# Two x loads merged on ScalarE, and the first transposes and gate projection put in order of landing, in a SwiGLU kernel

## Chip, cores, metric

One core of one Trainium2 chip. The metric is device time in microseconds (us). Quoted are medians of several executions. The kernel before took 164.04 us (164.0 to 164.34, three runs).

## The reference

```python
B, S, D, F = 1, 2048, 640, 1536            # bfloat16
def reference(x, w_gate, w_up, w_down):
    g = jax.nn.silu(x @ w_gate)
    u = x @ w_up
    return (g * u) @ w_down
```

## The kernel before

Rows are worked on in four blocks of 512. Projections need x transposed. Blocks 1 to 3 get it by a transposing DMA. Block 0 is in a hurry: its four 128-row chunks are loaded plainly, transposed on TensorE into PSUM and copied to SBUF by VectorE and ScalarE. Until the data is there TensorE runs "fillers", matmuls on a tile of ones that nobody reads.

```python
    queues = (nc.sync, nc.scalar)
    halves = ((0, KD // 2 + 1), (KD // 2 + 1, KD))        # k 0-2 on SyncE, 3-4 on ScalarE
    for c in (0, 1):
        for i, eng in enumerate(queues):
            load_x(eng, c + 2 * i, c + 2 * i + 1)         # SyncE: chunks 0, 1; ScalarE: 2, 3
    for dst, src in ((wg_sb, wg_v), (wu_sb, wu_v)):       # first 128 columns of the weights
        for eng, (k0, k1) in zip(queues, halves):
            eng.dma_start(out=dst[:, k0:k1, wslice(0, 1)], in_=src[:, k0:k1, wslice(0, 1)])
    load_w(nc.sync, wg_sb, wg_v, *W_CHUNKS[1])            # "second gate piece", columns 128-383
    # ... [cut: table load, second up piece, all other weights, transposing loads]

    def transpose_chunk(c, parts):
        for copy, tag, k0, k1 in parts:                   # po_a, po_b: two PSUM buffers each
            pt = psum.tile([P, k1 - k0, P], bf16, tag=tag, name="pt")
            # ... [cut: k1 - k0 TensorE transposes of x_sb[:, c] into pt]
            copy(out=xT[:, k0:k1, c_sl], in_=pt[:])

            if sb == 0 and fc == 0:                       # first column block of row block 0
                warm(N_WARM)                              # 18 fillers
                transpose_chunk(0, [(dve, "po_a", 0, KD)])
                transpose_chunk(2, [(dve, "po_b", 0, KD)])
                warm(N_GAP)                               # 4
                for c in (1, 3):
                    transpose_chunk(c, [(act, "po_a", 0, 2), (dve, "po_b", 2, KD)])
                warm(2)
                proj_pair(pg, wg_sb, fc, sb, 0)           # gate, chunks 0 and 2
                proj_pair(pg, wg_sb, fc, sb, 1)           # gate, chunks 1 and 3
                proj(pu, wu_sb, fc, sb, 0, S_BLK)         # up, all
            else:                                         # "second block" is fc == 1
                proj(pg, wg_sb, fc, sb, 0, S_BLK)
                proj(pu, wu_sb, fc, sb, 0, S_BLK)
            # ... [cut: silu on ScalarE, product on VectorE; then the down projection]
```

## Time and profile before

| | kernel before |
|---|---|
| median time | 164.04 us |
| span in the trace | 162.8 us |
| TensorE busy | 159.0 us (98%) |
| first gate projection starts | 5.05 us |
| second block starts | 7.25 us |

A line of the chain of waits gives start, length and what held the end at that time. A line of the timeline gives start, length, engine, source line, operation and count, and in square brackets the idle time before it with what ended it. The spacing of TensorE's instructions is read from such a line as (length minus the 0.22 to 0.31 us that one of them takes) over (count minus 1), or directly from the starts in the trace. From the second block on the matmuls follow each other without a gap, so what can change is when the second block starts. The prediction shows the lines.

### The profile page before, as it was taken

How to read it: one execution, taken by the hardware profiler on the slowest of the kernel's cores; microseconds unless marked ns; L12 is line 12 of the kernel's file. 1: busy time of each engine (PE TensorE's matmuls, PEld its weight loads, DVE VectorE, ACT ScalarE, POOL GpSimd, SP SyncE). 2: the span in 40 equal slices, each digit the busy share in tenths (PEclk: the TensorE clock that was granted, in tenths of full speed). 3: DMA queues.
4: the chain of work that ended last, by engine and by line, in shares of the span. 5: the costliest groups of instructions: out<-in, count | busy, mean ns of one | idle time of the engine just before them, and what ended most of it. 6: DMA issues, size and time to landing. Idle time of an engine off the chain costs nothing.

```text
span 162.8 us, 1869 instructions
## 1 busy us (share of the span) xinstructions
PE 159.0 (98%) x766; PEld 75.3 (46%) x781; DVE 37.9 (23%) x58; ACT 42.4 (26%) x72; POOL 0.6 (0%) x6
## 2 busy tenths in 40 slices
PE   8999999999999999999999999999999999999994
PEld 7644444444444444444444444444444444445442
DVE  2322333310022333311002333331001333332000
ACT  3322222112222222221222222221213222222121
POOL 1000000000000000000000000000000000000000
PEclk9999999999999999999999999999999999999999
DMA  7999999804100000003110000000320000000302
GB/s 214 244 327 328 361 236 226 161 9 80 45 32 0 0 0 0 4 0 34 64 64 0 2 4 0 0 0 5 60 68 32 0 0 0 0 0 4 56 33 72
DMA packets 26888, 11.26 MB, mean 69 GB/s; under 512 B 17664, under 2 KB 26880, under 8 KB 26880
## 3 DMA queue, kind: packets, MB, share of 16 engines
q1 hardware_dynamic: 17968, 10.16, 22.8%
q10 hardware_dynamic: 8912, 0.98, 3.9%
q8 instruction: 6, 0.10, 0.3%
q14 instruction: 2, 0.02, 0.0%
HBM read 6.55 MB, written 2.62 MB: 56 GB/s over the span
## 4 chain that ended last, share of the span: by engine, by line
PE 96%; DMA 2%; issue 1%; SPq 0%; DVE 0%
PE pu L134 31%; PE pg L134 31%; PE po_a L213 25%; PE po_t L189 6%; DMA x_sb<-in_x_dram 2%; PE pg L149 1%; PE pt L125 0%; PE po_b L226 0%; SPq L74 0%; DVE ot_b L234 0%; PE pw L103 0%
## 5 line engine op out<-in xcount | busy, mean ns | idle before, releaser
L134 PE MATMUL pu<-xT,wu_sb 128*128 128x512 bf16 x230 | 58.9, 379 | 0.5
L134 PE MATMUL pg<-xT,wg_sb 128*128 128x512 bf16 x235 | 58.4, 379 | 0.0
L181 DVE TENSOR_TENSOR aT<-sg,pu 128x512 bf16<-128x512 f32 x48 | 33.1, 689 | 100.5 <-PE pu L134 100.5
L180 ACT ACTIVATE sg<-pg 128x512 f32<-128x512 f32 x48 | 28.7, 597 | 71.1 <-PE pg L134 70.1
L213 PE MATMUL po_a<-wd_sb,aT 128*128 128x512 bf16 x188 | 41.9, 379 | 0.2
L134 PEld LDWEIGHTS <-wu_sb 128*128 128x128 bf16 x240 | 23.5, 98 | 28.1 <-DMA wu_sb<-in_w_up_dram 0.2
L134 PEld LDWEIGHTS <-wg_sb 128*128 128x128 bf16 x235 | 22.9, 98 | 27.8 <-DMA wg_sb<-in_w_gate_dram 0.4
L213 PEld LDWEIGHTS <-aT 128*128 128x128 bf16 x192 | 18.8, 98 | 22.6
L221 ACT CAST ot<-po_a 128x512 bf16<-128x512 f32 x16 | 9.4, 585 | 32.4 <-PE po_a L213 19.3
L189 PE MATMUL po_t<-aT,wd_sb 128*128 128x512 bf16 (+1 forms) x47 | 10.3, 365 | 0.1
L189 PEld LDWEIGHTS <-wd_sb 128*128 128x128 bf16 x48 | 4.7, 98 | 5.1
L198 ACT CAST ot_t<-po_t 128x512 bf16<-128x512 f32 (+1 forms) x4 | 2.2, 558 | 11.6 <-PE po_t L189 11.6
L199 DVE STREAM_TRANSPOSE ot_q<-ot_t 128x512 bf16<-128x512 bf16 (+1 forms) x4 | 2.7, 678 | 9.0 <-ACT ot_t L198 9.0
L103 PE MATMUL pw<-ones 128*128 128x128 bf16 x24 | 2.8, 289 | 0.4 <-DVE ones L78 0.4
L234 DVE CAST ot_b<-po_b 128x128 bf16<-128x128 f32 x1 | 0.3, 291 | 9.9 <-PE po_b L226 9.9
L103 PEld LDWEIGHTS <-ones 128*128 128x128 bf16 x24 | 2.3, 136 | 0.4 <-DVE ones L78 0.4
L130 DVE COPY xT<-pt 128x640 bf16<-128x640 bf16 (+1 forms) x4 | 1.6, 424 | 3.5 <-PE pt L125 3.5
L125 PE MATMUL pt<-ident,x_sb 128*128 128x128 bf16 x20 | 1.9, 262 | 0.5 <-DMA x_sb<-in_x_dram 0.5
L125 PEld LDWEIGHTS <-x_sb 128*128 128x128 bf16 x20 | 1.5, 119 | 0.9 <-DMA x_sb<-in_x_dram 0.9
L89 ACT ACT_TABLE_LOAD x1 | 1.3, 1283 | 2.0 <-issue 2.0
L149 PE MATMUL pg<-xT,wg_sb 128*128 128x256 bf16 x10 | 1.3, 272 | 0.0
L149 PEld LDWEIGHTS <-wg_sb 128*128 128x128 bf16 x10 | 0.9, 98 | 0.1
(11 smaller groups left out, 3.5 us busy)
## 6 DMA issues: line engine op xcount, KB each, us to landing
out_dram<-ot SPq DMA_DIRECT2D x16, 128.0 KB, 1.7
wd_sb<-in_w_down_dram SPq DMA_DIRECT2D x1, 1920.0 KB, 12.0
wg_sb<-in_w_gate_dram SPq DMA_DIRECT2D x3, 480.0 KB, 7.7
wu_sb<-in_w_up_dram SPq DMA_DIRECT2D x3, 480.0 KB, 8.1
out_dram<-ot_q ACTq DMA_DIRECT2D x12, 32.0 KB, 1.9
x_sb<-in_x_dram SPq DMA_DIRECT2D x2, 160.0 KB, 3.1
x_sb<-in_x_dram ACTq DMA_DIRECT2D x2, 160.0 KB, 3.3
wg_sb<-in_w_gate_dram SPq DMA_DIRECT2D x1, 320.0 KB, 4.4
```

The lines of the kernel that those rows point to most:

```text
L103: nc.tensor.matmul(pw[:, 0:P], lhsT=ones[:], rhs=ones[:], start=True, stop=True)
L125: nc.tensor.transpose(out=pt[:, kd - k0, :], in_=x_sb[:, c, kd * P : (kd + 1) * P], identity=ident[:],)
L130: copy(out=xT[:, k0:k1, c_sl], in_=pt[:])
L134: nc.tensor.matmul(ps[:, c0:c1], lhsT=w_sb[:, kd, fc * P : (fc + 1) * P], rhs=xT[:, kd, sb * S_BLK + c0 : sb * S_BLK + c1], start=(kd == 0 ...
L149: nc.tensor.matmul(pair(ps[:]), lhsT=w_sb[:, kd, fc * P : (fc + 1) * P], rhs=pair(xT[:, kd, sb * S_BLK : (sb + 1) * S_BLK]), start=(kd == ...
L180: nc.scalar.activation(sg[:], pg[:], ACT.Silu)
L181: nc.vector.tensor_tensor(out=aT[:, fc, s_sl], in0=sg[:], in1=pu[:], op=ALU.mult)
L189: nc.tensor.matmul(po_t[:], lhsT=wd_sb[:, kf, DA:D], rhs=aT[:, kf, sb * S_BLK : sb * S_BLK + n_t], start=(kf == 0), stop=(kf == KF - 1),)
L198: nc.scalar.copy(ot_t[:], po_t[:])
L199: nc.vector.transpose(out=ot_q[:], in_=ot_t[:])
L213: nc.tensor.matmul(po_a[:], lhsT=aT[:, kf, s0 : s0 + P], rhs=wd_sb[:, kf, 0:DA], start=(kf == 0), stop=(kf == KF - 1),)
L221: nc.scalar.copy(ot[:], po_a[:])
```

## The change

The intent: one load for chunks 2 and 3, so that they land together and early, and TensorE's work in the order in which the chunks then land, 0, 2, 3, 1. The first half of the gate projection covers chunks 2 and 3, the other half 0 and 1.

```diff
-    N_WARM, N_GAP = 18, 4
+    N_WARM, N_GAP = 18, 5
-    for c in (0, 1):
-        for i, eng in enumerate(queues):
-            load_x(eng, c + 2 * i, c + 2 * i + 1)
+    load_x(nc.sync, 0, 1)
+    load_x(nc.scalar, 2, SUB)
+    load_x(nc.sync, 1, 2)
... [cut: proj_pair removed]
                 transpose_chunk(0, [(dve, "po_a", 0, KD)])
+                warm(N_GAP)
                 transpose_chunk(2, [(dve, "po_b", 0, KD)])
-                warm(N_GAP)
-                for c in (1, 3):
+                for c in (3, 1):
                     transpose_chunk(c, [(act, "po_a", 0, 2), (dve, "po_b", 2, KD)])
                 warm(2)
-                proj_pair(pg, wg_sb, fc, sb, 0)
-                proj_pair(pg, wg_sb, fc, sb, 1)
+                proj(pg, wg_sb, fc, sb, 2 * P, S_BLK)
+                proj(pg, wg_sb, fc, sb, 0, 2 * P)
```

More of the change, by code (lines that the diff above doesn't have):

```diff
@@ L140, in proj @@
             )
-    def proj_pair(ps, w_sb, fc, sb, b):
-        def pair(ap):
-            return ap.rearrange("p (a b c) -> p b a c", b=2, c=P)[:, b]
-        for kd in range(KD):
-            nc.tensor.matmul(
-                pair(ps[:]),
-                lhsT=w_sb[:, kd, fc * P : (fc + 1) * P],
-                rhs=pair(xT[:, kd, sb * S_BLK : (sb + 1) * S_BLK]),
-                start=(kd == 0),
-                stop=(kd == KD - 1),
-            )
     for sb in range(NSB):
```

## The prediction

> **What bounds the kernel now.** I read the head of the page first, then the chain that ended last, then the first nine microseconds of that chain, the engine timelines and the issues of loads one by one.
>
> ```profile
> span 162.8 us, 1869 instructions
> PE 159.0 (98%) x766; PEld 75.3 (46%) x781; DVE 37.9 (23%) x58; ACT 42.4 (26%) x72; POOL 0.6 (0%) x6
> PE 96%; DMA 2%; issue 1%; SPq 0%; DVE 0%
> ```
>
> TensorE is the bound: 96% of the chain is matmuls. The change touches none of the 128x512 matmuls. It can only move the moment from which they run without a break. Everything at stake lies in the few per cent marked DMA, issue and the small TensorE lines. The chain, cut to 0 to 9 us (start, length, what):
>
> ```profile
> 0.46 3.87 DMA x_sb<-in_x_dram
> 4.33 0.05 issue
> 4.37 0.73 PE pt L125 x10
> 5.10 0.11 PE pw L103 x2
> 5.21 1.09 PE pg L149 x10
> 6.31 0.05 issue
> 6.36 1.03 PE pu L134 x4
> 7.39 1.12 PE pg L134 x5
> ```
>
> A load of x, issued at 0.46, lands at 4.33; ten transposes, two fillers and the first gate projection follow directly. So the head start is a chain of load, transposes, projection. The timeline of starts shows the same, and one thing more:
>
> ```profile
> 2.46 1.20 PE L125 MATMUL pt<-ident,x_sb 128*128 128x128 bf16 x10
> 3.50 0.39 PE L103 MATMUL pw<-ones 128*128 128x128 bf16 x4
> 4.37 0.73 PE L125 MATMUL pt<-ident,x_sb 128*128 128x128 bf16 x10 [0.49 <-DMA x_sb<-in_x_dram]
> 5.05 1.25 PE L149 MATMUL pg<-xT,wg_sb 128*128 128x256 bf16 x10
> 7.25 0.76 PEld L134 LDWEIGHTS <-wg_sb 128*128 128x128 bf16 x5 [0.35 <-DMA wg_sb<-in_w_gate_dram]
> 8.17 0.92 PEld L134 LDWEIGHTS <-wu_sb 128*128 128x128 bf16 x5 [0.16 <-DMA wu_sb<-in_w_up_dram]
> ```
>
> The first projection starts at 5.05. At 7.25 the second column block waits for its gate weights: undisturbed, it would begin at 5.05 + 10 x 0.109 + 5 x 0.216 = 7.22. So 0.03 us is already lost to the weights, and an earlier projection gains nothing beyond that unless these weights land earlier too. The next (up) weights have about 0.2 us to spare.
>
> When each load lands is its issue plus the last column here (one or two loads a window; x chunks 0, then 1 and 3, then the second gate and up pieces):
>
> ```profile
> x_sb<-in_x_dram SPq DMA_DIRECT2D x1, 160.0 KB, 2.4
> ...
> x_sb<-in_x_dram SPq DMA_DIRECT2D x1, 160.0 KB, 3.9
> x_sb<-in_x_dram ACTq DMA_DIRECT2D x1, 160.0 KB, 4.0
> ...
> wg_sb<-in_w_gate_dram SPq DMA_DIRECT2D x1, 320.0 KB, 4.4
> ...
> wu_sb<-in_w_up_dram SPq DMA_DIRECT2D x1, 320.0 KB, 4.9
> ```
>
> Chunk 0 lands at 2.4, chunk 2 (issued 0.12, 2.7) at 2.8, chunk 1 at 4.33, chunk 3 (issued 0.6) at 4.6. The first gate piece on SyncE (0.91 + 3.9) lands at 4.8, ScalarE's (1.03 + 4.0) at 5.0, the second gate piece (2.80 + 4.4) at 7.2, the second up piece (3.21 + 4.9) at 8.1. Why the gate piece is issued only at 2.80, when SyncE was free at 1.88, is in SyncE's own waits:
>
> ```profile
> SPq L71 <- DMA x_sb<-in_x_dram: 1.8, 2, 0.9
> ```
>
> The program of the kernel before hands its loads eight completion semaphores in turn. The ninth load, this gate piece, takes the first one again and waits for chunk 2, landed at 2.78; the eleventh waits for chunk 3 (4.60, issued 4.62). That is 0.9 us of the 1.8 each.
>
> **What the Trainium skill says.** "DMA: Bandwidth & Descriptors", section "Issuing engines are not separate DMA queues": loads from different engines run on the same 16 DMA engines and interleave; issuing from several saves only the sequencer's issue time. The trace agrees: the DMA share is 0.95 to 0.99 from 1.5 to 3.0 us at 300 to 330 GB/s, with both queues loaded. So one merged load moves no byte sooner by itself. Same page, "Why a DMA increments its semaphore by 16 and not by 1": a load has landed when the last of its engines has. In the landing records chunk 3's sixteen increments come between 3.22 and 4.60, so a merged load waits for the slowest engine over both chunks. "TensorE: Matmul & The Clock Gate", Part 1: about 3.4 us of activity precede full clock, and an idle window of that length loses it. Here the starts go from 107 ns apart to 56 at about 3.4 us; the longest gap after that, 0.65 us of starts, is far too short to matter. That holds for the change too.
>
> **The change part by part.**
>
> *Issues.* A 160 KB load costs ScalarE 0.40 to 0.45 us of issue; the merged load has 256 rows like the first gate piece of ScalarE, which cost 0.46. So one issue, about 0.4 us, is saved. ScalarE's first weights go out at about 0.6 instead of 1.03. The activation table load moves from 2.04 to about 1.6, off the path.
>
> *Semaphores, an unmentioned effect.* One load fewer stands before the second gate piece, so it becomes the eighth and gets an unused semaphore. It should go out at about 1.9 rather than 2.80. The second up piece becomes the ninth and probably waits for the merged load (near 3.7) instead of 3.21. Between 4.5 and 5.5 us the DMAs moved only 164 and 202 GB/s, against some 300 around it, while the first 512-byte rows of the gate piece trickled in. Filling part of that saves, as an estimate, 0.5 x (290 - 180) GB/s x 1 us = 55 KB, or 0.2 us of its landing: 7.2 becomes 7.0. Without this the rest could not pay.
>
> *Landing of x.* The bytes are the same 640 KB. If descriptors are made in order of issue (chunk 0, both of the merged load, chunk 1), the merged load gains on chunk 1. The first packets of the four x loads appear at about 1.0, 1.5, 2.0 and 2.5 us, which fits such an order. I put the merged load at L = 3.7 (possible 3.5 to 4.3) and chunk 1 at X = 4.4 (4.2 to 4.6): later for chunk 2 by 0.9, earlier for chunk 3 by the same.
>
> *TensorE.* Twenty transposes, and 20 + 5 fillers instead of 20 + 4. The one filler more lies at about 3.4, where TensorE waits anyhow: 0. The ten 128x256 matmuls stay ten at 109 ns. Chunk 0's transposes still start at 2.46. Three conditions now set the first projection's start:
> 1. The gate weights of SyncE: 4.8 plus 0.1 = 4.9.
> 2. Chunk 1: X + 0.05 + 5 x 0.056 + 3 x 0.056 = X + 0.49 = 4.89.
> 3. VectorE: it copies chunk 2 (491 ns) and chunk 3 (358 ns) after the merged load, where before chunk 2 was done by 4.19. Chunk 2's transposes end about 0.53 after L, its copy at L + 1.02, chunk 3's at about L + 1.38. The third matmul of the projection reads that, 0.22 us after the first: start at L + 1.17 = 4.87.
>
> The largest is 4.90, 0.15 us before today's 5.05. The end of that projection and the first up projection follow at 0.109 and 0.216 us a matmul; the second block then starts at 7.07, or at 7.05 by its weights. Against 7.25 that is a gain of 0.18, of which I keep 0.15. Nothing later has room to add to it: from there the matmuls follow each other.
>
> **The rivals.**
> - *Nothing moves.* The second gate weights land at 7.2 as before, because the DMA engines have the same bytes to move (the share is near 1 until 4.5 us), and TensorE waits longer at the second block. For it: the 0.35 us wait of the weight load. Against it: the dip and the freed semaphore. It makes 0 to 0.03 us, 164.0.
> - *The merged load lands late.* If the two queues share evenly to the end, L is 4.3 and condition 3 gives 5.47: 0.4 us lost, 164.4 us. For it: chunk 3 lands at 4.60 now. Against it: the order of first packets, and the author's order of transposes.
> - *The weights gain more.* If the earlier issue closes the whole dip, 0.37 us, and the first gate pieces also land earlier, 163.6 us.
>
> **Range and chances.** 164.04 - 0.15 = 163.9 us. The rivals span 163.6 to 164.4, and the three runs before lie 0.34 us apart; the range of 8 in 10 is 163.45 to 164.35. Two per cent is 3.3 us, more than the whole first wait for x beyond chunk 0 (4.6 - 2.4 = 2.2 us), so it is out of reach upwards; for a loss of that size the clock would have to fall back or a transfer stall. Chances: 0.01 faster, 0.98 within 2%, 0.01 slower.
>
> **What would show it.** The ScalarE load of 320 KB issued at 0.1 lands near 3.8; chunk 1 near 4.4. SyncE issues the second gate piece near 1.9, and its wait there for x is gone or moved to the up piece. The first 256-wide matmul starts near 4.9 with VectorE's copies in an unbroken row before it; the second block starts at about 7.1. The 128x512 groups keep their counts and their 379 ns. The prediction is wrong if the first projection starts after 5.1, if the second block still waits until 7.2, or if the row of 512-wide matmuls behind it breaks anywhere.

## The result

The changed kernel took 164.57 us (164.17 to 164.76, six runs) against 164.06 us (163.85 to 164.41, six runs) for the kernel before. The ratio is 1.0024 (95% interval 1.0007 to 1.004). Ratios are the mean time of one kernel's fast runs over that of the other's of the same rounds, so not quite the ratio of the medians. Within 2%, but above the predicted range, and with the opposite sign: 0.4 us lost where 0.15 us was to be gained.

The head of the page after, then its chain from 0 to 10 us:

```profile
span 163.3 us, 1870 instructions
...
0.12 3.59 DMA x_sb<-in_x_dram
3.71 0.05 issue
3.76 1.78 PE pt L125 x15
5.54 0.15 PE pw L103 x2
5.69 1.09 PE pg L134 x10
```

The merged load lands at 3.71, within 0.01 of the prediction. Fifteen transposes follow at once, but they take the time from 3.76 to 5.33. The timeline of TensorE after:

```profile
2.93 0.74 PE L103 MATMUL pw<-ones 128*128 128x128 bf16 x5
3.76 1.78 PE L125 MATMUL pt<-ident,x_sb 128*128 128x128 bf16 x15
5.33 0.36 PE L103 MATMUL pw<-ones 128*128 128x128 bf16 x2
5.53 1.25 PE L134 MATMUL pg<-xT,wg_sb 128*128 128x256 bf16 x10
7.70 0.59 PE L134 MATMUL pg<-xT,wg_sb 128*128 128x512 bf16 x2
```

Fifteen transposes in 1.78 us are (1.78 - 0.31) / 14 = 0.105 us apart; the ten before the projection of the kernel before took 0.73 us, (0.73 - 0.22) / 9 = 0.057. In the starts, the kernel before goes from 107 to 56 ns at 3.48 us (the prediction's "about 3.4"). This moment is called the rise from here on. In the changed kernel it comes at about 5.5. The second block starts at 7.70 in place of 7.25. To within 0.01 these 0.45 us are the difference of the two profiled times (164.57 and 164.13).

The loads after, in order merged, chunk 1, SyncE's first gate piece, second gate piece (last column: issue to landing), and SyncE's wait:

```profile
x_sb<-in_x_dram ACTq DMA_DIRECT2D x1, 320.0 KB, 3.6
...
x_sb<-in_x_dram SPq DMA_DIRECT2D x1, 160.0 KB, 3.8
...
wg_sb<-in_w_gate_dram SPq DMA_DIRECT2D x1, 96.0 KB, 4.3
...
wg_sb<-in_w_gate_dram SPq DMA_DIRECT2D x1, 320.0 KB, 4.9
...
SPq L71 <- DMA x_sb<-in_x_dram: 1.3, 1, 1.3
```

The second gate piece is issued at 1.92, not 2.80, and lands at 6.8 in place of 7.2: the freed semaphore works. The single wait left, 1.3 us, is that of the second up piece for the merged load, as predicted. But SyncE's first gate piece, issued at 0.91, lands at 5.24 by the landing records, where it was 4.85. Even at full clock the projection could not have started before about 5.29.

One more line, of the page before, shows what does not warn the reader:

```profile
PEclk9999999999999999999999999999999999999999
```

It shows full clock in the first slice (0 to 4.1 us), where TensorE ran at half rate up to 3.48 us. The clock records behind it (in the packed trace; no view prints them) begin with the rise, at 3.48 us here, and in the changed kernel's trace there are none. So the spacing of starts is the thing to read.

### The profile page after: what moved, and what is told of

It is laid out like the page before. It is cut to its first block, busy times and chain, and to the rows that moved or that the text cites. A ratio compares the mean times of both kernels' runs of the same rounds, so it can differ in the third digit from the quotient of the medians.

```text
span 163.3 us, 1870 instructions
## 1 busy us (share of the span) xinstructions
PE 159.9 (98%) x767; PEld 76.2 (47%) x782; DVE 37.9 (23%) x58; ACT 42.5 (26%) x72; POOL 0.6 (0%) x6
## 4 chain that ended last, share of the span: by engine, by line
PE 96%; DMA 2%; issue 1%; DVE 0%
PE pg L134 32%; PE pu L134 31%; PE po_a L198 25%; PE po_t L174 6%; DMA x_sb<-in_x_dram 2%; PE pt L125 1%; PE po_b L211 0%; DVE ot_b L219 0%; PE pw L103 0%
## 5 line engine op out<-in xcount | busy, mean ns | idle before, releaser
L134 PE MATMUL pg<-xT,wg_sb 128*128 128x512 bf16 (+1 forms) x245 | 59.6, 375 | 0.0
L198 PEld LDWEIGHTS <-aT 128*128 128x128 bf16 x192 | 18.8, 98 | 22.5
L125 PE MATMUL pt<-ident,x_sb 128*128 128x128 bf16 x20 | 2.5, 309 | 0.1
L125 PEld LDWEIGHTS <-x_sb 128*128 128x128 bf16 x20 | 2.0, 141 | 0.5 <-DMA x_sb<-in_x_dram 0.5
L130 ACT COPY xT<-pt 128x256 bf16<-128x256 bf16 x2 | 0.7, 372 | 1.8 <-PE pt L125 1.8
L211 PEld LDWEIGHTS <-aT 128*128 128x128 bf16 x12 | 0.8, 98 | 0.2
```

The costliest lines, as they stand in the source:

```text
L125: nc.tensor.transpose(out=pt[:, kd - k0, :], in_=x_sb[:, c, kd * P : (kd + 1) * P], identity=ident[:],)
L134: nc.tensor.matmul(ps[:, c0:c1], lhsT=w_sb[:, kd, fc * P : (fc + 1) * P], rhs=xT[:, kd, sb * S_BLK + c0 : sb * S_BLK + c1], start=(kd == 0 ...
L198: nc.tensor.matmul(po_a[:], lhsT=aT[:, kf, s0 : s0 + P], rhs=wd_sb[:, kf, 0:DA], start=(kf == 0), stop=(kf == KF - 1),)
```

## The experiments

Seventeen more runs were made: thirteen edited kernels, one of them twice, the changed kernel twice more and the kernel before once more. Two theories stood first. **Clock by gap:** TensorE's idle time from 3.47 to 3.76 us keeps its clock from rising. **Clock by chance:** the moment of the rise differs from execution to execution, whatever the kernel. Beside them, **weights**: SyncE's first gate piece lands later in the changed kernel, and that costs time at any clock.

### The changed kernel once more, and its parts

The changed kernel again, unedited:

> The changed kernel once more. In its first trace TensorE started its 128-wide instructions 107 ns apart up to about 5.5 us, where the kernel before went to 56 ns at about 3.4 us. Theory clock-gap (the rise to full clock is late because TensorE idles from 3.47 to 3.76 us, every time): again 107 ns up to about 5.5 us, first projection at 5.5, time near 164.5. Theory chance (the moment of the rise differs from execution to execution, whatever the kernel): another moment, and times that scatter over 0.5 us.

164.43 us (163.96 to 164.86), ratio 1.0005 (0.9984 to 1.0025). The kernel before, in the same session, took 163.94 to 164.79 in eleven runs. The loss of the first comparison is not there, and both kernels scatter by some 0.9 us. In the trace the rise came at about 5.5 us again, so this look alone decides nothing between the theories.

The merged load alone:

```diff
 # kernel before
-    for c in (0, 1): ... load_x(eng, c + 2 * i, c + 2 * i + 1)
+    load_x(nc.sync, 0, 1); load_x(nc.scalar, 2, SUB); load_x(nc.sync, 1, 2)
```

> The merged load alone, with the order of transposes and projections of the kernel before. Merged load lands at 3.7, chunk 1 at 4.3, SyncE's gate piece at 5.24 as in the changed kernel. Theory clock-gap: TensorE idles from 2.97 to 3.7, so full clock comes late too; 5 transposes, 4 fillers, 10 transposes, 2 fillers at 107 ns from 3.76 make the first projection start at about 6.0, time near 165.0. Theory weights (SyncE's gate piece landing at 5.24 instead of 4.85 holds the projection, clock or no clock): first projection at 5.3, time near 164.3.

164.85 us (164.03 to 166.11), ratio 1.0039 (1.0005 to 1.0072). Here TensorE idles longer (2.86 to 3.58), yet the rise came at 4.2, earlier than in the changed kernel. That speaks against the gap. In the look, SyncE's gate piece landed at 4.94 and the projection started at 5.15. The first theory's 6.0 and the second's 5.3 both missed. The interval lies above 1, but this kernel was measured in one session only, and its trace is of a short run: whether the merged load alone costs 0.4%, and what made the 166.11, stays open.

The order alone:

```diff
 # changed kernel
-    load_x(nc.sync, 0, 1); load_x(nc.scalar, 2, SUB); load_x(nc.sync, 1, 2)
+    for c in (0, 1): ... load_x(eng, c + 2 * i, c + 2 * i + 1)
```

> The new order of transposes, fillers and half projections alone, with the four x loads of the kernel before. Chunk 2 is there at 2.8, so TensorE has no gap before 3.5 us. Theory clock-gap: full clock at about 3.4 us; chunk 3 (lands 4.6) is then transposed from 4.65, chunk 1 after it, first projection at about 5.35, time near 164.35. Theory chance: the rise at any moment between 3.4 and 6 us.

164.6 us (163.98 to 164.99), ratio 1.0013 (0.9989 to 1.0036). TensorE had no gap from chunk 0's landing up to 4.4, but the rise came at 4.4, not at 3.4: against the gap again. Chunk 3 landed at 3.85 here, where the one trace that the prediction rests on had 4.60.

The gap filled:

```diff
 # changed kernel
-    N_WARM, N_GAP = 18, 5
+    N_WARM, N_GAP = 18, 8
```

> The changed kernel with 8 fillers in place of 5 between chunk 0 and chunk 2, which fills TensorE's gap from 3.47 to 3.76 us. Theory clock-gap: full clock at about 3.4 us as in the kernel before; transposes of the other chunks at 56 ns, all done by about 4.6. Then theory weights says that the first projection waits for SyncE's gate piece (5.24) and starts at 5.3: 164.3. Without theory weights it would start at 4.8 and the time be 163.8. Theory chance: no different from the changed kernel, 164.5.

164.28 us (163.91 to 164.92), ratio 1.0001 (0.998 to 1.0022). Its timeline:

```profile
2.84 1.06 PE L103 MATMUL pw<-ones 128*128 128x128 bf16 x8
3.69 1.81 PE L125 MATMUL pt<-ident,x_sb 128*128 128x128 bf16 x15
```

The fillers now run up to the transposes without a gap, and the fifteen transposes are still 107 ns apart; the rise came at 5.8. The gap theory is refuted.

### Holding the loads back until the clock is up

If the clock is taken out of the comparison, what is left is the change itself. A row of VectorE work should hold all loads back while TensorE runs fillers (later fillers doubled):

```diff
 # kernel before, changed kernel, and the latter with the edit of the candidate below
+    hold = consts.tile([P, S_BLK], f32); nc.vector.memset(hold[:], 1.0)
+    for _ in range(12): nc.vector.tensor_tensor(out=hold[:], in0=hold[:], in1=hold[:], op=ALU.mult)
+    nc.vector.memset(x_sb[:, :, 0:2], 0.0)
-    N_WARM = 18
+    N_WARM = 124
```

> The kernel before with all loads held back by about 8 us of VectorE work while TensorE runs 124 fillers, so that TensorE is at full clock before the first x chunk lands; later fillers doubled in number. Theory chance (the rise to full clock comes at a moment that differs from execution to execution, and this makes the scatter of 0.9 us in the times): no 107 ns spacing once x has landed, and the times of the fast runs agree within 0.3 us. Rival (the scatter is of the transfers): they scatter as before, over 0.8 us. Second block from 7.25 us after the first load's issue, held by its gate weights.

> The changed kernel held back in the same way, so at full clock too. Theory weights (SyncE's gate piece lands 5.2 us after the first issue in place of 4.85, and that alone holds the first projection): first projection 5.3 us after the first load's issue, second block at 7.45 without a wait for its own weights, time 0.2 us above the gated kernel before. Rival (the clock was all of the loss): first projection at 4.9, second block at 7.07, time 0.15 us below the gated kernel before, as first predicted.

> The gated changed kernel with the first gate block as one load on ScalarE behind the merged load, and the first up block as one load on SyncE. Theory weights: the gate block lands at about 4.9 after the first issue, first projection at about 5.0, second block at about 7.15: 0.3 us below the gated changed kernel and 0.1 below the gated kernel before. Rival (something else holds the projection, such as VectorE's copies): no earlier than in the gated changed kernel.

These three failed as experiments: the write to `x_sb` does not depend on `hold`, was scheduled ahead of it, and the loads went at 0.8 us. TensorE's 124 fillers then set the start of the transposes (9.2 to 9.8 us in the traces). Times 170.28, 170.2 and 170.78 us, ratios to the kernel before 1.0357, 1.0362 and 1.0372. They say nothing on the cost of the change, but their traces are used twice below.

Mended, with the write reading `hold`, ten multiplications and 140 fillers, so that loads go at 8.24 us:

```diff
-    nc.vector.memset(x_sb[:, :, 0:2], 0.0)
+    nc.vector.tensor_copy(out=x_sb[:, :, 0:2], in_=hold[:, 0:8].rearrange("p (a b) -> p a b", b=2))
```

> The kernel before with the hold mended (the first attempt let the loads go at 0.8 us, since the write that should hold them ran ahead of the row of VectorE work): loads go at about 8 us, TensorE has 140 fillers first and is at full clock when x lands. Theory chance (the moment of the clock's rise makes the scatter): fast runs within 0.3 us of each other, where the kernel before scatters over 0.9. Rival (transfers scatter): 0.8 us as ever. First projection about 5.05 and second block about 7.25 us after the first load's issue.

> The changed kernel held in the same way, at full clock. Theory weights (SyncE's gate piece lands at 5.2 after the first issue in place of 4.85 and holds the first projection even at full clock): first projection at 5.3, second block at 7.45, time 0.2 us above the held kernel before. Rival (the clock was all of the loss): first projection at 4.9, second block at 7.07, 0.15 us below the held kernel before.

> The held changed kernel with the first gate block as one load on ScalarE and the first up block as one load on SyncE. Theory weights: gate block lands at 4.95, first projection at 5.0, second block at 7.2: 0.25 us below the held changed kernel, about 0.05 below the held kernel before. Rival (VectorE's copies hold it): no gain on the held changed kernel.

Medians 172.37, 172.62 and 172.65 us; ratios to the kernel before 1.0487 (1.0463 to 1.0512), 1.0505 (1.048 to 1.0531) and 1.051 (1.0477 to 1.0542). In the order expected between the first two, 0.25 us apart, but the intervals overlap. The third, which puts the gate block on ScalarE, brought nothing: in its trace that block landed 5.19 us after the first issue, not 4.95. So the case that it was to test, the gate weights landing early, did not come about.

Four of the five runs of the first lie within 0.20 us of each other, and five of the six of the second within 0.22 us. One run of each is 0.5 to 0.7 us slower; of the third, five of six lie within 0.39 us and one 1.3 us above them. The kernel before, whose clock was left to chance, covered 164.02 to 164.99 us in the same session. Over all runs the expected 0.3 us was missed (0.71, 0.80 and 1.73 us); without the slow run of each, the first two meet it. With so few runs it is likely, not shown, that holding the clock up takes most of the everyday scatter away. What made the slow runs is known for one alone: the trace of the first happened to be its slow run, and there the second gate piece landed 7.7 us after the first issue, not 7.2. Its projection started 5.10 us after the first issue, that of the changed kernel's look 5.09.

What the six traces do show is the rise itself. Up to their first transposes TensorE does the same in all of them: fillers, back to back, from 0.26 or 0.27 us. The three failed runs, then the three mended ones:

```profile
0.27 9.21 PE L108 MATMUL pw<-ones 128*128 128x128 bf16 x124 [0.27 <-DVE ones L78]
0.26 9.66 PE L108 MATMUL pw<-ones 128*128 128x128 bf16 x124 [0.26 <-DVE ones L78]
0.27 9.14 PE L107 MATMUL pw<-ones 128*128 128x128 bf16 x124 [0.27 <-DVE ones L78]
...
0.26 9.39 PE L110 MATMUL pw<-ones 128*128 128x128 bf16 x140 [0.26 <-DVE ones L78]
0.27 9.68 PE L110 MATMUL pw<-ones 128*128 128x128 bf16 x140 [0.27 <-DVE ones L78]
0.26 10.33 PE L109 MATMUL pw<-ones 128*128 128x128 bf16 x140 [0.26 <-DVE ones L78]
```

The same 124 fillers take 9.14 to 9.66 us and the same 140 take 9.39 to 10.33. In the starts the rise comes at 4.8, 5.7 and 4.6 us, and at 3.25, 3.9 and 5.2. There is no gap and no transpose among these fillers, so neither sets the moment.

The chain of the held changed kernel (loads go at 8.25), then TensorE's weight loads for the last fillers and for the projection, show what holds it at full clock:

```profile
11.82 0.47 PE pt L132 x5
...
12.31 0.50 DVE xT L137
...
12.85 0.33 PE pt L132 x3
...
13.40 1.20 PE pg L141 x10
...
12.96 0.26 PEld L110 LDWEIGHTS <-ones 128*128 128x128 bf16 x4
13.34 0.99 PEld L141 LDWEIGHTS <-wg_sb 128*128 128x128 bf16 x10
```

Chunk 2's transposes, VectorE's copy of them, and only then the last three transposes of chunk 1. Those need a buffer `po_b`, of which there are two, holding chunks 2 and 3. So the merged load's landing (11.77) reaches the projection by way of a full PSUM buffer. This path was ready for the projection at 13.24 (the last filler started at 13.18, and they are 0.056 apart), 1.47 us after the landing. The projection's weights came last: SyncE's gate piece landed at 13.29, 5.04 us after the first issue, and the projection started at 13.34. The second and third failed runs, whose loads had all landed, show the buffer's wait alone: 12.01 - 10.60 = 11.49 - 10.08 = 1.41 us from chunk 2's first transpose to the projection (the lines of the second run follow). With 0.05 from landing to transpose that is 1.46, or 1.35 with two fillers in place of four. In the first profile of the kernel before neither of the two set the start.

```profile
10.60 0.83 PE L130 MATMUL pt<-ident,x_sb 128*128 128x128 bf16 x12
...
11.62 0.33 PE L130 MATMUL pt<-ident,x_sb 128*128 128x128 bf16 x3 [0.19 <-DVE xT L135]
...
12.01 1.26 PE L139 MATMUL pg<-xT,wg_sb 128*128 128x256 bf16 x10
```

### A candidate, and the fillers ahead of the projection

```diff
 # changed kernel: candidate
-    for dst, src in ((wg_sb, wg_v), (wu_sb, wu_v)): ... [two loads each, split by k]
+    load_w(nc.scalar, wg_sb, wg_v, 0, 1)
+    load_w(nc.sync, wu_sb, wu_v, 0, 1)
-                warm(2)
```

> A candidate, not gated: the changed kernel with the gate block on ScalarE and the up block on SyncE, and without the two fillers ahead of the first projection. If the weights cost 0.3 us and the two fillers 0.2 us at half clock, its time is 0.2 to 0.3 us below the changed kernel and 0.1 to 0.2 us below the kernel before, about 0.999 of it, within the scatter of single runs.

164.28 us (164.03 to 164.43), ratio 0.9982 (0.9967 to 0.9996): as hoped. It was run again, with a third run of the changed kernel:

> The candidate once more: gate block on ScalarE, up block on SyncE, no fillers ahead of the first projection. It was 0.9982 of the kernel before. If its gain is real (fewer instructions at half clock after the last landing): 0.998 to 0.9995 and less scatter than the kernel before; if it was luck: 1.000.

164.37 us (164.08 to 164.74), ratio 1.001 (0.9992 to 1.0028). An interval that excludes 1 by a hair, from five runs against eleven, did not survive a second session.

> The changed kernel a third time, to see whether the 0.24% of the first comparison stands. Theory draw (the moment of the clock's rise decides most of a run's time, and the first six against six had luck in it): ratio to the kernel before between 0.999 and 1.002, interval over 1. Rival (the change costs 0.4 us whatever the clock does): 1.0024 again, interval clear of 1.

164.2 us (164.0 to 164.8), ratio 1.0002 (0.9984 to 1.0021). So three comparisons gave 1.0024, 1.0005 and 1.0002. In this look the rise came at 6.3, the latest for a kernel with its 18 fillers; five of the 128x256 matmuls of the projection ran at half rate too:

```profile
3.46 1.79 PE L125 MATMUL pt<-ident,x_sb 128*128 128x128 bf16 x15
...
5.25 1.78 PE L134 MATMUL pg<-xT,wg_sb 128*128 128x256 bf16 x10
```

The kernel before without the two fillers ahead of its projection:

```diff
 # kernel before
-                warm(2)
```

> The kernel before without its two fillers ahead of the first projection. Where the clock is up by then they cost 0.11 us and hide in the wait for the gate weights; where it is not they cost 0.21 us. So 0 to 0.2 us below the kernel before, mean 0.1, ratio 0.9990 to 1.0. If it does as well as the candidate, the merged load has no part in the candidate's gain.

164.38 us (163.81 to 165.04), ratio 1.0003 (0.9982 to 1.0024): no gain that can be seen. Its look shows another source of scatter, the landing of the second gate piece:

```profile
8.16 1.04 PE L134 MATMUL pg<-xT,wg_sb 128*128 128x512 bf16 x4 [0.39 <-DMA wg_sb<-in_w_gate_dram]
```

The second gate piece landed at 8.11 in this execution, and the second block stood waiting for it; without that it would have started at about 7.61 (its up projection's last start, 7.39, plus 0.216). It is the slowest of the six runs.

The kernel before, once more:

> The kernel before, one more look at the moment of the clock's rise. Theory chance: not 3.4 us again but anywhere from 3.4 to 6.8; where it comes after 5.4, the first projection starts at 5.7 and the time is 164.7 or more. Rival (fixed by the kernel): 3.4 us again.

```profile
2.52 1.25 PE L125 MATMUL pt<-ident,x_sb 128*128 128x128 bf16 x10
...
4.20 1.24 PE L125 MATMUL pt<-ident,x_sb 128*128 128x128 bf16 x10
...
5.39 1.26 PE L149 MATMUL pg<-xT,wg_sb 128*128 128x256 bf16 x10
...
7.56 0.81 PE L134 MATMUL pg<-xT,wg_sb 128*128 128x512 bf16 x3
```

The same program as in the first profile, and its second ten transposes take 1.24 us in place of 0.73. The rise came at 5.3, the projection at 5.39, the second block at 7.56, and the time was 164.42 us. The moment does not belong to the kernel. Nor does it to the chip: in eight looks on one chip it lay between 4.2 and 5.8.

### A late clock on purpose

Without the 18 first fillers TensorE's first work is chunk 0's transposes, at about 2.4 us. In the first profile the rise came 3.1 us after TensorE's first instruction (0.40 to 3.48); an estimate from that is a rise at 5.5 or later here.

```diff
 # kernel before, and changed kernel
-    N_WARM = 18
+    N_WARM = 0
```

> The kernel before without its 18 first fillers, so that TensorE's first work is the transposes of chunk 0 at 2.4 us[...]. Theory clock (a late rise makes the long times): all 20 transposes 107 ns apart, first projection at 5.7, its 128x256 matmuls 213 ns apart until the rise, second block at 7.9 to 9.5, times 164.8 to 166.4, none below 164.7. Rival (the scatter comes from the transfers alone, the clock is hidden): 164.0 to 164.8 as before.

> The changed kernel without its 18 first fillers. Theory clock: TensorE then does 15 transposes and 2 fillers at 107 ns from the merged load's landing (3.5 to 3.7), first projection at 5.3 to 5.5, 0.2 us before the kernel before under the same handicap, so times 164.6 to 166.2, ratio of the two about 0.999, with a wide interval. If instead the change costs 0.4 us at any clock, it lies 0.4 us above the other.

The first took 165.05 us (164.89 to 165.9), ratio 1.0032 (1.0006 to 1.0058), with no run below 164.89, where the kernel before in the same session went from 164.14 to 165.13. The second took 164.6 us (164.39 to 165.89), ratio 1.002 (0.9987 to 1.0054). Rises at 7.2 and 5.45, 4.7 and 3.0 us after TensorE's first instruction. Without its fillers the kernel before never had a short time, as a late clock demands. The changed kernel under the same handicap showed no loss against the kernel before; the ratio of the two ratios, 0.9988, is the one expected, but well inside the intervals. In the first one's chain (0 to 18 us) the half rate reaches the projection:

```profile
4.16 1.07 PE pt L125 x10
5.22 0.21 PE pw L103 x2
5.44 2.00 PE pg L149 x10
```

### All looks together

| kernel | rise to full rate | projection starts | second block starts | time of that run | time minus second block |
|---|---|---|---|---|---|
| before | 3.5 | 5.05 | 7.25 | 164.13 | 156.88 |
| before, second | 5.3 | 5.39 | 7.56 | 164.42 | 156.86 |
| before, no fillers ahead of projection | 5.9 | 5.00 | 8.16 | 165.04 | 156.88 |
| before, no first fillers | 7.2 | 5.23 | 8.35 | 165.23 | 156.88 |
| changed | 5.5 | 5.53 | 7.70 | 164.57 | 156.87 |
| changed, second | 5.5 | 5.32 | 7.59 | 164.46 | 156.87 |
| changed, third | 6.3 | 5.25 | 7.94 | 164.80 | 156.86 |
| changed, 8 fillers | 5.8 | 5.51 | 7.83 | 164.69 | 156.86 |
| changed, no first fillers | 5.45 | 5.28 | 7.54 | 164.39 | 156.85 |
| loads only | 4.2 | 5.15 | 7.32 | 164.19 | 156.87 |
| order only | 4.4 | 5.10 | 7.27 | 164.15 | 156.88 |
| candidate | 4.6 | 5.02 | 7.20 | 164.03 | 156.83 |
| candidate again | 4.05 | 5.07 | 7.24 | 164.08 | 156.84 |

The last column is the same to 0.05 us in thirteen looks at nine programs. So the start of the second block decides the time, and that goes, first, with the moment of the rise: no look with a rise up to 4.6 is above 164.19 us, and none with a later one below 164.39. The eleven looks with the 18 fillers have rises from 3.5 to 6.3 us.

## Why the prediction was wrong, point by point

- *Merged load at 3.7, chunk 1 at 4.4.* Right: 3.71 and 4.26; over six looks at the merged load with split gate pieces, 3.41 to 3.71 and 3.96 to 4.26. What was wrong is the base. The kernel before's last x chunk landed at 4.60 in the profile used, and at 3.85 to 4.39 in four other looks with its four loads. Much of the head start to be gained was a late landing in one execution.
- *Freed semaphore.* Right in kind, small in size: issued at 1.92; landed at 6.54 to 6.81 in six looks against 7.00 to 8.11 in five with four x loads. The prediction had 7.0 against 7.2. The second block never waited for it in the changed kernel.
- *Condition 1, SyncE's first gate piece at 4.8.* Failed. It was taken over from the profile before; it landed at 5.24. Over the looks it averages 5.01 (4.70 to 5.24, six) against 4.84 (4.77 to 4.91, five). ScalarE's first pieces, sent 0.45 us sooner, land sooner (4.60 for 5.06) and this one later. The prediction counted the one as a gain and did not reckon the other; that the other comes of it is likely, but no run isolates it. With the average, 5.01 + 0.05 = 5.06, nothing is left of the gain on 5.05, at any clock.
- *Condition 2, X + 0.49.* **This is the step that failed most.** It gave 4.89, and 5.53 was measured. (Its own terms sum to 0.50 and not 0.49, and those of condition 3 to 1.16 and not 1.17: a hundredth, without weight.) It reckoned 56 ns for each transpose and filler, because the trace showed the rise at about 3.4 us, "That holds for the change too". The rise came at 5.5, and fifteen transposes and two fillers at 107 ns reach from 3.76 to 5.53. The kernel before itself rises elsewhere in other executions. The 3.4 us also seemed to agree with the page that was cited, by chance: TensorE's first instruction is at 0.40, so its activity before the rise was 3.1 us.
- *Condition 3, L + 1.17.* Failed in a term left out: chunk 1's last transposes wait for a PSUM buffer until chunk 2 is copied. Measured at full clock, L + 1.46 with four fillers ahead of the projection, so 1.35 with two, in place of 1.17. With the L of 3.7 that is 5.05 and not 4.87: this too would have taken the gain.
- *The largest is 4.90.* It was 5.53. Of the 0.45 us between the two profiled runs, worked out from them: 5.29 (gate piece plus 0.05) less 5.05 is 0.24 for the weights, 5.53 less 5.29 is 0.24 for the clock, less 0.03 for the wait for its own weights that fell away. At a rise later than 5.3 the kernel before pays for the clock as well, so the second term is a draw and not the change's.
- *Range.* It allowed for three runs 0.34 us apart. In the later sessions the kernel before covers 0.85 to 1.0 us. The kernel before's own median moved between 164.06 and 164.66 from session to session. A half width of 0.45 us around one median was too narrow for that alone.
- *Rivals.* None of the three named the clock, though the argument had cited the page that has it. "The merged load lands late" came closest in time (164.4) by a mechanism that did not occur.

What is left of the change: nothing that these runs resolve. Two sessions of three have it within 0.05% of the kernel before, with intervals of 0.2% to each side. The first, 0.24% slower with an interval clear of 1, was not reproduced. That it was only the draw of clock and landings is likely, not shown: its six runs have one trace. A real cost of up to 0.17 us at an early rise, an estimate from the gate piece's averages (5.01 less 4.84), fits the held pair's 0.25 us within its intervals, but was not separated from zero. No version beat both kernels.

## What to carry to other kernels

A head of some 5 us whose TensorE work starts cold is partly a lottery: look at several traces of the unchanged kernel before reckoning a gain of a few tenths from one. Read the rate from the spacing of starts, not from the clock row. When loads are re-ordered to bring one forward, follow the one that falls behind, and every buffer that the new order fills twice.

## What the Trainium skill lacked or had wrong

- "TensorE: Matmul & The Clock Gate", Part 1, has the rise to full clock vary by 500 ns either way, with a free-running window of 3.4 us behind it; beside that it calls the count of slow matmuls variable from run to run. In eleven looks at kernels with the same first 18 fillers from 0.40 us on, the rise came from 3.5 to 6.3 us, a spread of 2.8 us, and in six with longer rows of fillers from 3.25 to 5.7. The spread fits a window of that length whose phase is left to chance; the earliest rises, 3.0 us after TensorE's first instruction, are shorter than a whole one. No run here shows the window itself.
- The same page, Part 4, says that full clock does not engage for transposes. Here the transposes (MATMULs in the trace, which does not tell their mode) sped up with the rest: the second ten of the kernel before took 0.73 us (56 ns apart) after the rise, and 1.24 us (107 ns apart) in an execution with a late one. In the changed kernel without first fillers most of TensorE's work before the rise was transposes, and the rise still came 3.0 us after the first of them.
- That page's Part 1 warns that the clock's trace events are unreliable, but no page says in what way here: the kernel before's clock records begin at 3.48 us, the changed kernel's trace has none, and both give a mean granted clock of 1.000 in spite of the half rate before the rise.
- No page gives the scatter of one load's landing between executions of like loads: the second gate piece landed at 7.00, 7.17, 7.20, 7.27 and 8.11 us with four x loads ahead of it.
